# Windowed attention and feed-forward on one core: chunks of 384 tokens, split zero fill and a new order of work

## The chip, the core and the metric

One core of a Trainium2 chip runs the whole computation. Its engines are TensorE (PE in the profile; its weight loads are PEld), VectorE (DVE), ScalarE (ACT) and GpSimd (POOL); DMA queues are started by SyncE (SP) and ACT. The metric is device time in microseconds. Before the change it is 338.51 us, the median of three runs (337.94 to 339.54). Runs are compared in the fast state only, unless a slow one is named as such. "Granted clock" is the share of TensorE's full clock that the trace records.

## The reference

```python
# q, k, v: 8 batches x 8 heads x 576 tokens x 64, fp32; w_in 512 x 2048, w_out 2048 x 512
scores = scale * q @ k.T
rel    = pos[:, None] - pos[None, :]
plain  = (rel >= 0) & (rel < 32)                        # heads 0 to 3
dil    = (rel >= 0) & (rel < 128) & (rel % 4 == 0)      # heads 4 to 7
attn   = softmax(where(mask, scores, -1e9))
x      = (attn @ v).transpose(0, 2, 1, 3).reshape(4608, 512)
h      = x @ w_in
out    = maximum(0.01 * h, h) @ w_out                   # 4608 x 512, fp32
```

## The kernel before

The kernel is a list of steps, `PROGRAM`, and a loop that emits the instructions of each step. No scheduler reorders them: every engine gets its own share of the list in that order, with waits for data and buffers. In the trace ACT's 276 exponentials, logarithms and evictions start in just that order. The steps that matter here:

- `lq`, `lv`, `lw` load q and k, v, and a quarter of a weight matrix; `cq`, `cv`, `cw` cast them to fp16 on DVE (`V`), ACT (`A`) or GpSimd (`P`).
- `B` transposes q and k on PE; `T` does it by DMA (from group 5 on).
- `S:u` computes the scores of attention unit `u` and their exponential; `M:u` multiplies by the mask (a step `S:u:b` adds a bias on PE instead); `D:u` computes values and denominators and writes the normalised result to xT.
- `I:c:j` is one tile of the first feed-forward layer of token chunk `c`; `O:t:g` is a quarter of the second layer of 128-token tile `t`.
- `Z:n` multiplies a zero tile n times: fillers where the author expected PE to wait.

There are 16 groups of three units: half a batch (four heads) in two units of two heads x 384 tokens, and one unit of four heads x the last 192 tokens.

```python
psa = ...tile_pool(name="psa", bufs=1, space=PSUM)    # sps (2 banks), o, den
psm = ...tile_pool(name="psm", bufs=4, space=PSUM)    # tag pm: hp, op, tp
CHUNKS = [(0, 384), (384, 192), (576, 448)] + [(1024 + 512 * i, 512) for i in range(7)]
RING = 2048       # tokens that xT holds
GRING = 1024      # tokens that gt holds
...
def values(u, log_recip=False, pool=None):
    if pool is None:
        o   = psa.tile([128, 512], FP32, tag="o")
        den = psa.tile([128, 512], FP32, tag="den")
    else:                                  # "p": borrow two of the four pm banks
        den = pool.tile([128, 512], FP32, tag="pm")
        o   = pool.tile([128, 512], FP32, tag="pm")
    ...                                    # den matmuls, o matmuls
    if log_recip:                          # "l": logarithm, then exponential, on ACT
        nc.scalar.activation(out=ln, in_=den, func=AF.Ln)
        nc.scalar.activation(out=rec, in_=ln, func=AF.Exp, scale=-1.0)
    else:                                  # "r"
        nc.vector.reciprocal(out=rec, in_=den)
    ...                                    # xT = o * rec on DVE, cut in two where the ring wraps

def ff_in(c, j):
    hp = psm.tile([128, 512], FP32, tag="pm")
    for i in range(4):
        nc.tensor.matmul(hp[:, 0:w], w1[j // 4][:, i, j % 4::4], xT[:, i, x0:x0 + w], ...)
    nc.scalar.activation(out=gt[:, j, g0:g0 + w], in_=hp[:, 0:w], func=AF.Prelu, alpha=0.01)

def ff_out(t, g):                          # the tile stays open from g == 0 to g == 3
    if g == 0:
        ops[t] = psm.tile([128, 512], FP32, tag="pm")
    for j in range(4 * g, 4 * g + 4):
        nc.tensor.matmul(ops[t], gt[:, j, g0:g0 + 128], w2[g][:, j % 4, :], ...)
    if g == 3:
        nc.scalar.copy(out=ob, in_=ops[t])
        nc.scalar.dma_start(out[128 * t:128 * t + 128, :], ob)
```

The softmax here doesn't subtract the row's maximum and nothing guards it: scores larger than these inputs give would overflow.

## Time and profile before

| | before |
|---|---|
| time | 338.51 us |
| span of the profiled run (whose time is 339.5 us) | 337.6 us |
| PE, ACT, DVE, POOL busy | 97%, 51%, 51%, 28% |
| filler matmuls | 59, 21.8 us busy |
| first feed-forward matmul at | 27.4 us |
| first second-layer matmul at | 76.4 us |
| DMA busy in the first 28 us, and from 28 to 64 us | 93%, 96% |

PE is nearly always busy, so its stream decides the time. The question to put to such a profile isn't whether PE is busy but with what. Fillers count as busy, and the prediction takes them apart. One view more belongs here: the timeline of PE just before the first group of chunk 2 (start, length, engine, line, operation, tiles, count, and in brackets the wait).

```profile
57.07 0.35 PE L281 MATMUL den<-em,ones 80*64 80x384 f16 x2 [0.62 <-DVE em L265]
...
58.59 0.82 PE L396 MATMUL wp<-xT 128*128 128x512 f16 x2
59.47 0.35 PE L281 MATMUL den<-em,ones 128*64 128x384 f16 x2
...
61.26 0.35 PE L281 MATMUL den<-em,ones 128*64 128x384 f16 x2
61.80 0.36 PE L289 MATMUL o<-em,vh 128*64 128x96 f16 x8 [0.18 <-DVE xT L313]
...
62.37 1.47 PE L396 MATMUL wp<-xT 128*128 128x512 f16 x4
63.68 1.11 PE L343 MATMUL hp<-xT,w 128*128 128x448 f16 x5
```

Between 56.5 and 63.7 us PE has little real work. The last three attention units of chunk 2 (11, 9 and 8) stand there one behind the other in the single pair of banks `o` and `den`, some 2 us apart, and the product of the last one ends at 63.4 us. It isn't their values that are late: those had landed by 38.6 us and were cast by 44.2. At that moment not one second-layer matmul has been issued, although chunks 0 and 1 have gone through the first layer; the quarter of w_out that the program uses first lands last, at 62.6 us.

### The profile page before, as it was taken

Reading aid. Unit: us, or ns where it says so; the run is one execution under the profiler, and the core shown is the slowest. Engines: PE = TensorE matmul, PEld = TensorE weight load, DVE = VectorE, ACT = ScalarE, POOL = GpSimd, SP = SyncE. Lnnn points to the kernel's source line nnn. Section 1 sums busy time; section 2 is a strip of 40 time slices with the busy share of each in tenths; the row PEclk is TensorE's granted clock in tenths of the full one; section 3 lists DMA queues with packets and bytes.
Section 4 is the critical chain, followed back from the end, with each engine's and each line's share of the span. In section 5 each row is a group of like instructions: output and inputs, shape, how many; then the busy total and the mean of one; then the engine's idle time right before and its main releaser. Section 6 shows DMA issues by size and latency. Waiting matters only on the chain.

```text
span 337.6 us, 6297 instructions
## 1 busy us (share of the span) xinstructions
PE 326.7 (97%) x2639; PEld 168.6 (50%) x2639; DVE 173.0 (51%) x190; ACT 171.3 (51%) x293; POOL 95.0 (28%) x93
## 2 busy tenths in 40 slices
PE   7999898999999899999999999999999999999995
...
DMA  6999899790499399999669945700110020011011
GB/s 208 287 392 376 285 292 337 177 193 31 135 261 283 86 234 242 227 288 222 155 166 242 212 107 162 174 3 0 64 62 2 8 85 33 0 62 64 0 57 67
DMA packets 111243, 53.02 MB, mean 157 GB/s; under 512 B 96880, under 2 KB 101488, under 8 KB 110704
## 3 DMA queue, kind: packets, MB, share of 16 engines
...
## 4 chain that ended last, share of the span: by engine, by line
PE 90%; DVE 5%; issue 1%; DMA 1%; ACT 1%; DVEq 0%
PE op L353 36%; PE hp L343 34%; PE wp L396 6%; PE sps L255 6%; PE den L281 4%; PE o L289 2%; PE tp L206 2%; DVE rec L297 2%; DVE em L265 2%; DMA out_dram<-ob 1%; DVE xT L313 1%; PE sps L243 1%; ACT ln L294 0%; ACT ob L357 0%; DVE vh L189 0%
## 5 line engine op out<-in xcount | busy, mean ns | idle before, releaser
L343 PE MATMUL hp<-xT,w 128*128 128x512 f16 (+3 forms) x640 | 130.9, 359 | 0.0
L353 PE MATMUL op<-w,gt 128*128 128x512 f16 x576 | 128.8, 379 | 0.0
L345 ACT ACTIVATE gt<-hp 128x512 f16<-128x512 f32 (+3 forms) x160 | 88.0, 554 | 43.0 <-PE hp L343 42.3
L297 DVE RECIPROCAL rec<-den 128x384 f32<-128x384 f32 x32 | 81.8, 2557 | 42.5 <-PE den L281 42.5
L343 PEld LDWEIGHTS <-w 128*128 128x128 f16 x640 | 68.9, 114 | 52.8 <-issue 1.2
L353 PEld LDWEIGHTS <-gt 128*128 128x128 f16 x576 | 54.9, 98 | 64.6
L357 ACT COPY ob<-op 128x512 f32<-128x512 f32 x36 | 21.1, 587 | 82.3 <-PE op L353 82.3
L313 DVE TENSOR_TENSOR xT<-o,rec 128x192 f16<-128x192 f32 (+3 forms) x72 | 34.6, 508 | 34.1 <-ACT rec L295 30.8
L258 ACT ACTIVATE er<-sps 128x768 f16<-128x768 f32 (+1 forms) x48 | 38.8, 808 | 24.0 <-PE sps L255 21.9
L265 DVE TENSOR_TENSOR em<-er,mask 128x768 f16<-128x768 f16 (+1 forms) x42 | 30.8, 736 | 2.2 <-ACT er L258 2.2
L396 PE MATMUL wp<-xT 128*128 128x512 f16 x59 | 21.8, 420 | 3.2 <-DVE xT L112 1.3
L189 POOL CAST vh<-vf 128x2048 f16<-128x2048 f32 (+1 forms) x8 | 13.5, 1682 | 39.5 <-PE o L289 21.6
L176 POOL CAST qh<-qf 96x768 f16<-96x768 f32 x16 | 14.3, 921 | 36.2 <-DMA qf<-in_q_dram 35.9
L255 PEld LDWEIGHTS <-kT 64*128 64x128 f16 (+1 forms) x448 | 14.8, 121 | 17.0 <-issue 16.1
L255 PE MATMUL sps<-qT,kT 64*128 64x96 f16 (+1 forms) x448 | 22.9, 229 | 0.0
L176 POOL CAST kh<-kf 96x768 f16<-96x768 f32 x20 | 17.6, 904 | 5.0 <-DMA kf<-in_k_dram 4.3
L289 PEld LDWEIGHTS <-vh 128*64 128x64 f16 (+1 forms) x448 | 15.8, 110 | 3.4 <-DVE xT L313 0.7
L281 PE MATMUL den<-em,ones 128*64 128x384 f16 (+1 forms) x84 | 14.8, 349 | 2.4 <-DVE em L265 2.2
L185 POOL CAST vh<-vf 128x1536 f16<-128x1536 f32 x6 | 9.0, 1503 | 28.1 <-PE o L289 22.8
L330 POOL CAST w<-wf 128x2048 f16<-128x2048 f32 x7 | 13.9, 1983 | 7.4 <-DMA wf<-in_moe_w_out_dram 4.3
L289 PE MATMUL o<-em,vh 128*64 128x96 f16 (+1 forms) x392 | 14.8, 201 | 0.6 <-DVE xT L313 0.6
L281 PEld LDWEIGHTS <-ones 128*64 128x64 f16 (+1 forms) x96 | 5.7, 106 | 11.0 <-issue 6.7
...
## 6 DMA issues: line engine op xcount, KB each, us to landing
...
```

Of the source, the lines that this page charges most:

```text
L176: eng(out=t[0:96, 12 * D * p:12 * D * p + 12 * D].rearrange("p (t h d) -> p h t d", t=6, h=2), in_=f[0:96, 12 * p:12 * p + 12, :].rearrang ...
L255: nc.tensor.matmul(sps[0:kp, hh, w * x:w * x + w], ka, qa, start=not pe_mask, stop=not pe_mask or x == len(tiles) - 1)
L258: nc.scalar.activation(out=er[0:kp], in_=sps[0:kp, :, 0:384], func=AF.Exp, scale=SCALE)
L265: nc.vector.tensor_tensor(out=em[0:kp].rearrange("p h (t c) -> p h t c", c=w), in0=er[0:kp].rearrange("p h (t c) -> p h t c", c=w), in1=ba ...
L281: nc.tensor.matmul(den[64 * hh:64 * hh + 64, 0:384], ones[0:kp], em[0:kp, hh, :], start=True, stop=True)
L289: nc.tensor.matmul(o[64 * hh:64 * hh + 64, w * x:w * x + w], vt[0:kp, sl, :], em[0:kp, hh, w * x:w * x + w], start=True, stop=True)
L297: nc.vector.reciprocal(out=rec, in_=den[:, 0:384])
L313: nc.vector.tensor_tensor(out=out_x, in0=ins[0], in1=ins[1], op=ALU.mult)
L343: nc.tensor.matmul(hp[:, 0:w], w1[j // 4][:, i, j % 4::4], xT[:, i, x0:x0 + w], start=(i == 0), stop=(i == 3))
L345: nc.scalar.activation(out=gt[:, j, g0:g0 + w], in_=hp[:, 0:w], func=AF.Prelu, alpha=0.01)
L353: nc.tensor.matmul(op, gt[:, j, g0:g0 + 128], w2[g][:, j % 4, :], start=(j == 0), stop=(j == 15))
L396: nc.tensor.matmul(wp, warm[:, 0:128], warm, start=True, stop=True)
```

## The change

Its intent: chunks of 384 tokens instead of 512, with xT as a ring of exactly four batches so that no product is cut at the wrap; the zero fill of buffers split over engines; and the whole list of steps laid out again, by an author who wanted it to hold up under several assumptions about durations.

```diff
-CHUNKS = [(0, 384), (384, 192), (576, 448)] + [(1024 + 512 * i, 512) for i in range(7)]
-RING = 2048
-GRING = 1024
+CHUNKS = [(0, 384), (384, 192), (576, 384), (960, 192)] + [(1152 + 384 * i, 384) for i in range(9)]
+RING = 2304
+GRING = 1152
 PROGRAM (cut to the part between chunk 1 and chunk 2):
-I:1:15 D:11:l Z:1 S:14:m Z:1 Z:1 D:9:l S:13:m Z:1 Z:1 cv:4:P:b cq:5:k:P:b D:8:l S:12:m
-Z:2 cw:1:0:P Z:1 Z:1 I:2:0
+D:6:lp M:11 D:8:lp D:7:r S:10:m O:0:0 I:1:7 ... I:1:12 M:10 I:1:13 lv:3:b lw:1:3 O:1:0 O:0:1
+O:1:1 cv:3:V:b I:1:14 lq:4:b O:2:0 O:2:1 ... I:1:15 cq:4:k:P:b O:0:2 D:11:l O:1:2 ... O:0:3
+D:10:l O:1:3 O:2:2 B:4:0:AV D:9:l B:4:1:VV S:12:m ... T:5 O:2:3 O:3:0 I:2:0
 ... (the rest of PROGRAM is all new)
-    qT = [cst.tile([128, PAD + 2 * S], FP16) ...]
+    qT = [cst.tile([128, 2 * S], FP16) ...]
-    nc.vector.memset(vf[0][0:32], 0.0)
-    for h in range(4):
-        nc.vector.memset(vf[1][64:128, 8 * h + 4:8 * h + 8, :], 0.0)
+    nc.vector.memset(vf[1].rearrange(...)[64:128, :, 1, :], 0.0)
+    nc.scalar.copy(out=vf[0][0:32]..., in_=warm[0:32]...)            # zeros, on ACT
+        nc.vector.memset(t[:, S:PAD + S], 0.0)                      # for each kT
     values(): the loop over the two pieces of a wrapped product is gone
```

Counted over the list: fillers 59 to 35; first-layer groups 160 to 208, second-layer groups 144 in both; units with a DVE reciprocal 32 to 9; units that borrow `pm` banks for values 4 to 21; value casts on GpSimd 14 of 18 to 7 of 16; weight casts on GpSimd 7 of 8 to 3 of 8.

More of the change, by code (lines that the diff above doesn't have):

```diff
@@ L19 @@
 NTOK = B * S
-CHUNKS = [(0, 384), (384, 192), (576, 448)] + [(1024 + 512 * i, 512) for i in range(7)]
-RING = 2048
-GRING = 1024
+CHUNKS = [(0, 384), (384, 192), (576, 384), (960, 192)] + [(1152 + 384 * i, 384) for i in range(9)]
+RING = 2304
+GRING = 1152
 NEG = -30000.0
 PROGRAM = """
-Z:2 Z:2 mask Z:1 lq:1:0 Z:2 Z:1 Z:1 lq:0:0 cq:0:q:V:0 Z:2 lv:1:0 Z:1 lq:1:1 Z:1 lq:0:1 cq:0:k:A:0
-cq:1:k:P:0 Z:4 lv:0:0 cv:1:P:0 Z:2 B:0:0:VA Z:1 cq:1:k:P:1 lv:0:1 Z:1 cq:1:q:V:0 lw:0:0 cq:1:q:V:1
-Z:1 cq:0:k:P:1 cq:0:q:P:1 lv:1:1 lq:2:b Z:1 S:0:b cv:1:P:1 lq:3:b Z:2 cw:0:0:P B:1:0:AA Z:3 Z:1
@@ L30 @@
-cv:0:V:0 Z:1 lw:0:1 S:3:b B:0:1:VA cq:3:k:P:b cw:0:1:P B:1:1:AV cv:0:V:1 Z:1 Z:2 lw:0:2 S:1:b Z:2
-Z:1 D:3:lp S:4:b Z:1 D:0:lp cw:0:2:P D:1:lp Z:3 lw:0:3 S:2:b D:4:lp cq:2:q:A:b Z:2 S:5:b Z:1 Z:1
-cq:2:k:V:b Z:1 lv:2:b I:0:0 lv:3:b lq:4:b I:0:1 I:0:2 B:2:0:AA cq:3:q:V:b B:2:1:AV cw:0:3:P Z:1 Z:1
-D:5:l B:3:0:VA S:6:m lw:1:1 Z:1 Z:1 I:0:3 Z:1 B:3:1:VA lw:1:2 S:9:m D:2:l cv:3:P:b I:0:4 M:6
-cv:2:V:b I:0:5 I:0:6 S:10:m I:0:7 M:9 I:0:8 I:0:9 lq:5:b I:0:10 lv:4:b M:10 I:0:11 I:0:12 I:0:13
-I:0:14 S:7:m D:6:r I:0:15 M:7 I:1:0 I:1:1 cq:4:q:P:b I:1:2 I:1:3 I:1:4 cq:4:k:V:b I:1:5 cw:1:1:P
@@ L36 @@
-S:8:m I:1:6 cw:1:2:P I:1:7 I:1:8 lw:1:3 I:1:9 D:7:l lw:1:0 I:1:10 S:11:m lq:6:b B:4:0:VV D:10:l M:11
-I:1:11 B:4:1:AV I:1:12 I:1:13 M:8 I:1:14 I:1:15 D:11:l Z:1 S:14:m Z:1 Z:1 D:9:l S:13:m Z:1 Z:1
-cv:4:P:b cq:5:k:P:b D:8:l S:12:m Z:2 cw:1:0:P Z:1 Z:1 I:2:0 I:2:1 cq:5:q:V:b T:5 lv:5:b cq:6:k:P:b
-I:2:2 I:2:3 I:2:4 I:2:5 I:2:6 I:2:7 I:2:8 I:2:9 lv:6:b M:12 I:2:10 I:2:11 cw:1:3:V D:12:r cv:5:P:b
-I:2:12 I:2:13 I:2:14 I:2:15 O:0:0 O:0:1 O:0:2 O:0:3 O:1:0 O:1:1 M:14 O:1:2 O:1:3 O:2:0 S:16:m D:14:l
@@ L41 @@
-O:2:1 M:13 O:2:2 cq:6:q:V:b T:6 lq:7:b O:2:3 O:3:0 O:3:1 S:17:m M:16 M:17 D:16:l lq:8:b O:3:2 O:3:3
-S:15:m D:13:l O:4:0 O:4:1 M:15 O:4:2 O:4:3 O:5:0 cv:6:P:b O:5:1 O:5:2 O:5:3 O:6:0 D:15:l S:18:m
-O:6:1 lv:7:b O:6:2 lv:8:b O:6:3 O:7:0 M:18 O:7:1 cq:7:k:V:b S:19:m D:18:r cv:7:V:b O:7:2 O:7:3 I:3:0
-M:19 I:3:1 D:17:l I:3:2 cq:7:q:A:b T:7 lq:9:b lv:9:b I:3:3 I:3:4 S:20:m D:19:r M:20 cq:8:q:P:b
-cq:8:k:P:b cv:8:P:b I:3:5 I:3:6 I:3:7 I:3:8 I:3:9 S:21:m D:20:r M:21 T:8 I:3:10 I:3:11 I:3:12 I:3:13
-I:3:14 S:22:m D:21:r M:22 lq:10:b lv:10:b I:3:15 O:8:0 O:8:1 O:8:2 O:8:3 S:23:m D:22:r M:23
@@ L47 @@
-cq:9:q:P:b cq:9:k:P:b cv:9:P:b O:9:0 O:9:1 O:9:2 O:9:3 O:10:0 S:24:m D:23:r M:24 T:9 O:10:1 O:10:2
-O:10:3 O:11:0 S:25:m D:24:r M:25 lq:11:b lv:11:b O:11:1 O:11:2 O:11:3 I:4:0 I:4:1 S:26:m D:25:r M:26
-cq:10:q:P:b cq:10:k:P:b cv:10:P:b I:4:2 I:4:3 I:4:4 I:4:5 I:4:6 S:27:m D:26:r M:27 T:10 I:4:7 I:4:8
-I:4:9 I:4:10 I:4:11 S:28:m D:27:r M:28 lq:12:b lv:12:b I:4:12 I:4:13 I:4:14 I:4:15 O:12:0 S:29:m
-D:28:r M:29 cq:11:q:P:b cq:11:k:P:b cv:11:P:b O:12:1 O:12:2 O:12:3 O:13:0 S:30:m D:29:r M:30 T:11
@@ L52 @@
-O:13:1 O:13:2 O:13:3 O:14:0 O:14:1 S:31:m D:30:r M:31 lq:13:b lv:13:b O:14:2 O:14:3 O:15:0 O:15:1
-O:15:2 S:32:m D:31:r M:32 cq:12:q:P:b cq:12:k:P:b cv:12:P:b O:15:3 I:5:0 I:5:1 I:5:2 I:5:3 S:33:m
-D:32:r M:33 T:12 I:5:4 I:5:5 I:5:6 I:5:7 I:5:8 S:34:m D:33:r M:34 lq:14:b lv:14:b I:5:9 I:5:10
-I:5:11 I:5:12 S:35:m D:34:r M:35 cq:13:q:P:b cq:13:k:P:b cv:13:P:b I:5:13 I:5:14 I:5:15 O:16:0
-O:16:1 S:36:m D:35:r M:36 T:13 O:16:2 O:16:3 O:17:0 O:17:1 O:17:2 S:37:m D:36:r M:37 lq:15:b lv:15:b
-O:17:3 O:18:0 O:18:1 O:18:2 O:18:3 S:38:m D:37:r M:38 cq:14:q:P:b cq:14:k:P:b cv:14:P:b O:19:0
@@ L58 @@
-O:19:1 O:19:2 O:19:3 I:6:0 S:39:m D:38:r M:39 T:14 I:6:1 I:6:2 I:6:3 I:6:4 S:40:m D:39:r M:40 I:6:5
-I:6:6 I:6:7 I:6:8 I:6:9 S:41:m D:40:r M:41 cq:15:q:P:b cq:15:k:P:b cv:15:P:b I:6:10 I:6:11 I:6:12
-I:6:13 I:6:14 S:42:m D:41:r M:42 T:15 I:6:15 O:20:0 O:20:1 O:20:2 S:43:m D:42:r M:43 O:20:3 O:21:0
-O:21:1 O:21:2 O:21:3 O:22:0 S:44:m D:43:r M:44 O:22:1 O:22:2 O:22:3 O:23:0 S:45:m D:44:r M:45 O:23:1
-O:23:2 O:23:3 I:7:0 I:7:1 S:46:m D:45:r M:46 I:7:2 I:7:3 I:7:4 I:7:5 I:7:6 S:47:m D:46:r M:47 I:7:7
@@ L63 @@
-I:7:8 I:7:9 I:7:10 D:47:r I:7:11 I:7:12 I:7:13 I:7:14 I:7:15 O:24:0 O:24:1 O:24:2 O:24:3 O:25:0
-O:25:1 O:25:2 O:25:3 O:26:0 O:26:1 O:26:2 O:26:3 O:27:0 O:27:1 O:27:2 O:27:3 I:8:0 I:8:1 I:8:2 I:8:3
-I:8:4 I:8:5 I:8:6 I:8:7 I:8:8 I:8:9 I:8:10 I:8:11 I:8:12 I:8:13 I:8:14 I:8:15 O:28:0 O:28:1 O:28:2
-O:28:3 O:29:0 O:29:1 O:29:2 O:29:3 O:30:0 O:30:1 O:30:2 O:30:3 O:31:0 O:31:1 O:31:2 O:31:3 I:9:0
-I:9:1 I:9:2 I:9:3 I:9:4 I:9:5 I:9:6 I:9:7 I:9:8 I:9:9 I:9:10 I:9:11 I:9:12 I:9:13 I:9:14 I:9:15
-O:32:0 O:32:1 O:32:2 O:32:3 O:33:0 O:33:1 O:33:2 O:33:3 O:34:0 O:34:1 O:34:2 O:34:3 O:35:0 O:35:1
@@ L69 @@
-O:35:2 O:35:3
+Z:3 lq:1:1 Z:8 lq:0:1 Z:2 cq:0:q:V:1 cq:1:k:A:1 Z:1 lq:0:0 lq:1:0 cq:1:q:P:1 lv:1:b Z:3 cq:0:k:A:1
+B:1:1:VV Z:5 cq:0:q:V:0 Z:1 B:0:1:AA cq:1:k:P:0 Z:2 cq:1:q:V:0 Z:2 S:4:b B:1:0:VA lv:0:b lq:2:b
+S:1:b lw:0:0 Z:1 cv:1:V:b cq:0:k:P:0 lq:3:b B:0:0:AA lw:0:1 S:3:b D:4:rp S:0:b D:3:lp cq:2:q:V:b Z:3
+S:2:b Z:1 cv:0:P:b lw:0:2 D:0:lp cq:2:k:P:b D:1:l S:5:b B:2:1:AV B:2:0:VA cq:3:k:V:b Z:2 D:2:lp
+cw:0:0:P lw:0:3 lv:2:b Z:1 cq:3:q:P:b S:7:m D:5:l mask S:6:m cw:0:1:V lw:1:0 I:0:0 I:0:1 M:7
@@ new lines @@
+B:3:0:AA S:8:m B:3:1:AV I:0:2 I:0:3 S:9:b I:0:4 cw:0:2:V I:0:5 I:0:6 M:6 I:0:7 S:11:m M:8 I:0:8
+I:0:9 I:0:10 cw:0:3:V lw:1:1 I:0:11 I:0:12 I:0:13 cv:2:P:b cw:1:0:V I:0:14 I:0:15 cw:1:1:P lw:1:2
+I:1:0 I:1:1 I:1:2 I:1:3 I:1:4 cw:1:2:P I:1:5 I:1:6 D:6:lp M:11 D:8:lp D:7:r S:10:m O:0:0 I:1:7 I:1:8
+I:1:9 I:1:10 I:1:11 I:1:12 M:10 I:1:13 lv:3:b lw:1:3 O:1:0 O:0:1 O:1:1 cv:3:V:b I:1:14 lq:4:b O:2:0
+O:2:1 cq:4:q:P:b cw:1:3:V lv:4:b lq:5:b I:1:15 cq:4:k:P:b O:0:2 D:11:l O:1:2 lq:6:b O:0:3 cq:6:q:P:b
@@ new lines @@
+D:10:l O:1:3 O:2:2 B:4:0:AV D:9:l B:4:1:VV S:12:m cq:5:q:V:b cq:5:k:V:b T:5 O:2:3 O:3:0 I:2:0 I:2:1
+I:2:2 I:2:3 I:2:4 I:2:5 I:2:6 I:2:7 S:14:m I:2:8 I:2:9 I:2:10 I:2:11 cv:4:A:b cq:6:k:V:b O:3:1
+I:2:12 lv:5:b T:6 M:14 O:3:2 I:2:13 M:12 lq:7:b O:3:3 I:2:14 lv:6:b cv:5:P:b I:2:15 I:3:0 I:3:1
+I:3:2 O:4:0 I:3:3 I:3:4 S:13:m I:3:5 I:3:6 O:4:1 I:3:7 I:3:8 I:3:9 M:13 I:3:10 I:3:11 I:3:12 I:3:13
+S:15:m D:12:r D:13:lp O:5:0 cq:7:q:P:b M:15 O:4:2 I:3:14 S:16:m M:16 cq:7:k:P:b T:7 lv:7:b lq:8:b
+lq:9:b D:14:l O:5:1 O:4:3 S:17:m D:16:lp D:15:l I:3:15 cv:7:P:b M:17 O:5:2 O:6:0 O:6:1 I:4:0 O:5:3
@@ new lines @@
+I:4:1 S:19:m O:6:2 O:7:0 O:7:1 O:6:3 O:7:2 I:4:2 I:4:3 D:17:l S:20:m cq:9:k:P:b O:8:0 I:4:4 S:18:m
+I:4:5 M:20 O:8:1 I:4:6 O:7:3 O:8:2 S:21:m I:4:7 cv:6:V:b I:4:8 M:18 M:19 D:20:lp S:22:m M:21 D:18:r
+I:4:9 I:4:10 O:8:3 I:4:11 I:4:12 I:4:13 M:22 cq:8:k:V:b D:19:lp S:23:m D:22:lp D:21:l I:4:14 I:4:15
+O:9:0 O:10:0 I:5:0 O:9:1 O:9:2 cq:8:q:V:b T:8 lv:8:b O:9:3 I:5:1 I:5:2 O:11:0 O:10:1 I:5:3 O:11:1
+I:5:4 O:10:2 I:5:5 I:5:6 M:23 O:10:3 cq:9:q:P:b T:9 lq:10:b lq:11:b lv:9:b I:5:7 I:5:8 S:25:m D:23:l
@@ new lines @@
+I:5:9 O:11:2 I:5:10 I:5:11 I:5:12 I:5:13 I:5:14 M:25 I:5:15 I:6:0 I:6:1 O:12:0 I:6:2 O:12:1 S:26:m
+O:11:3 I:6:3 I:6:4 I:6:5 cv:8:V:b I:6:6 S:28:m O:12:2 O:12:3 S:24:m cq:10:q:P:b I:6:7 I:6:8 I:6:9
+O:13:0 cq:11:q:A:b I:6:10 I:6:11 O:13:1 M:28 S:27:m cq:11:k:P:b D:25:r I:6:12 I:6:13 cq:10:k:A:b
+T:10 lv:10:b I:6:14 O:13:2 cv:9:P:b lv:11:b T:11 lq:12:b lq:13:b I:6:15 O:14:0 O:13:3 O:14:1 M:24
+O:15:0 D:28:l S:29:m M:27 O:14:2 O:14:3 O:16:0 cq:12:k:P:b O:15:1 D:27:l D:24:lp S:30:m O:16:1
+O:15:2 O:15:3 I:7:0 I:7:1 I:7:2 I:7:3 I:7:4 M:29 I:7:5 I:7:6 cv:10:P:b O:16:2 cq:12:q:P:b T:12
@@ new lines @@
+lv:12:b lq:15:b M:26 O:16:3 O:17:0 M:30 S:33:m D:29:lp D:26:l cv:11:V:b lv:13:b S:34:m M:33 I:7:7
+O:17:1 I:7:8 I:7:9 I:7:10 I:7:11 M:34 I:7:12 I:7:13 I:7:14 D:33:r S:32:m cq:13:q:A:b O:17:2 D:34:lp
+S:31:m O:17:3 M:31 I:7:15 O:18:0 O:18:1 D:30:lp D:31:l S:35:m M:35 O:18:2 O:19:0 O:18:3 I:8:0 I:8:1
+I:8:2 I:8:3 I:8:4 cq:13:k:P:b T:13 lq:14:b S:38:m I:8:5 I:8:6 I:8:7 I:8:8 I:8:9 O:19:1 I:8:10 I:8:11
+I:8:12 O:19:2 I:8:13 I:8:14 I:8:15 M:32 O:20:0 S:36:m M:38 D:35:rp D:32:l S:37:m O:19:3 O:20:1
+O:20:2 cv:12:V:b cv:13:P:b M:37 O:21:0 O:20:3 O:22:0 cq:14:q:V:b cq:15:k:A:b M:36 O:21:1 O:22:1
@@ new lines @@
+I:9:0 I:9:1 D:38:l S:40:m O:21:2 I:9:2 M:40 O:21:3 I:9:3 cq:15:q:P:b T:15 lv:14:b I:9:4 I:9:5 I:9:6
+D:37:l D:40:rp S:39:m O:22:2 I:9:7 S:41:m D:36:l I:9:8 O:22:3 O:23:0 I:9:9 O:23:1 cq:14:k:P:b T:14
+lv:15:b I:9:10 O:23:2 M:39 I:9:11 O:23:3 D:39:l S:47:m I:9:12 I:9:13 I:9:14 I:9:15 M:41 I:10:0
+I:10:1 O:24:0 O:24:1 M:47 I:10:2 S:46:m I:10:3 O:24:2 I:10:4 O:25:0 S:45:m cv:15:V:b D:41:l D:47:lp
+S:42:m O:25:1 I:10:5 cv:14:V:b O:25:2 I:10:6 M:42 M:46 O:24:3 I:10:7 I:10:8 M:45 I:10:9 S:43:m
+D:45:lp D:46:l O:26:0 M:43 I:10:10 O:25:3 I:10:11 I:10:12 S:44:m D:43:r D:42:lp I:10:13 O:26:1
@@ new lines @@
+I:10:14 I:10:15 O:26:2 O:26:3 I:11:0 I:11:1 I:11:2 O:27:0 I:11:3 I:11:4 I:11:5 I:11:6 M:44 O:27:1
+O:27:2 O:27:3 D:44:lp I:11:7 I:11:8 O:28:0 I:11:9 I:11:10 I:11:11 O:29:0 I:11:12 O:28:1 I:11:13
+O:29:1 O:28:2 I:11:14 I:11:15 O:29:2 O:28:3 I:12:0 I:12:1 I:12:2 I:12:3 O:30:0 O:30:1 O:29:3 I:12:4
+O:30:2 O:31:0 O:30:3 I:12:5 I:12:6 I:12:7 I:12:8 I:12:9 I:12:10 O:32:0 O:31:1 I:12:11 I:12:12 O:31:2
+I:12:13 O:31:3 O:32:1 I:12:14 I:12:15 O:33:0 O:32:2 O:34:0 O:32:3 O:33:1 O:34:1 O:35:0 O:33:2 O:34:2
@@ L70 @@
+O:33:3 O:35:1 O:34:3 O:35:2 O:35:3
 """
@@ L115 @@
     NPE = 5
-    qT = [cst.tile([128, PAD + 2 * S], FP16, name=f"qT{i}") for i in range(NB)]
+    qT = [cst.tile([128, 2 * S], FP16, name=f"qT{i}") for i in range(NB)]
     kT = [cst.tile([128, PAD + 2 * S], FP16, name=f"kT{i}") for i in range(NB)]
@@ L121 @@
     vf = [cst.tile([128, 24, D], FP32, name="vf0"), cst.tile([128, 32, D], FP32, name="vf1")]
+    nc.vector.memset(vf[1].rearrange("p (h a r) d -> p h a (r d)", a=2, r=4)[64:128, :, 1, :], 0.0)
+    nc.scalar.copy(out=vf[0][0:32].rearrange("p (a t) d -> p a (t d)", a=3),
+                   in_=warm[0:32].unsqueeze(1).to_broadcast([32, 3, 512]))
     for t in kT:
         nc.vector.memset(t[:, 0:PAD], 0.0)
-    nc.vector.memset(vf[0][0:32], 0.0)
+        nc.vector.memset(t[:, S:PAD + S], 0.0)
     nc.vector.memset(vf[1][0:32], 0.0)
-    for h in range(4):
-        nc.vector.memset(vf[1][64:128, 8 * h + 4:8 * h + 8, :], 0.0)
     def rows_ap(x, off, ap):
@@ L195, in transpose @@
         for nm, dst in (("q", qT), ("k", kT)):
-            o = dst[n % NB][:, PAD:PAD + 2 * S].rearrange("p (c r) -> p c r", r=96)
+            o = dst[n % NB][:, -2 * S:].rearrange("p (c r) -> p c r", r=96)
             nc.sync.dma_start_transpose(o, qkh[n, nm][0:96, :])
@@ L206, in pe_transpose @@
                 nc.tensor.transpose(tp[r, 64 * t:64 * t + 64], h[r, t, :], ident[r, r])
-        o = (qT if nm == "q" else kT)[n % NB][:, PAD + S * p:PAD + S * p + S]
+        o = (qT if nm == "q" else kT)[n % NB][:, -2 * S:][:, S * p:S * p + S]
         eng(out=o.rearrange("p (r t) -> p r t", t=9),
@@ L250, in scores @@
                     ka = kT[n % NB][r, tok - 128 + j: tok - 128 + j + 4 * kp - 3: 4]
-                    qa = qT[n % NB][r, tok + j: tok + j + 4 * w - 3: 4]
+                    qa = qT[n % NB][r, tok - PAD + j: tok - PAD + j + 4 * w - 3: 4]
                 else:
                     ka = kT[n % NB][r, tok + 96 * j - 32: tok + 96 * j + 96]
-                    qa = qT[n % NB][r, tok + 96 * j: tok + 96 * j + 96]
+                    qa = qT[n % NB][r, tok - PAD + 96 * j: tok - PAD + 96 * j + 96]
                 nc.tensor.matmul(sps[0:kp, hh, w * x:w * x + w], ka, qa, start=not pe_mask,
```

19 lines of the change are left out of this document (6 added, 13 removed).

## The prediction

> **What bounds the kernel now.** I read the engine totals first, then the slices of the span, then the chain that ended last in order of time, then groups by form, and last the timeline of PE. Engine totals and two rows of the slices:
>
> ```profile
> PE 326.7 (97%) x2639; PEld 168.6 (50%) x2639; DVE 173.0 (51%) x190; ACT 171.3 (51%) x293; POOL 95.0 (28%) x93
> ...
> PE   7999898999999899999999999999999999999995
> ...
> DMA  6999899790499399999669945700110020011011
> ```
>
> PE has work almost everywhere, and the other engines are half idle, so PE's stream sets the end. The holes in PE's row lie in the first fifth, where DMA is full. But 97% busy isn't 97% useful. The groups by form (busy, mean of one, idle before):
>
> ```profile
> L353 PE MATMUL op<-w,gt 128*128 128x512 f16 x576 | 128.8, 379 | 0.0
> L343 PE MATMUL hp<-xT,w 128*128 128x512 f16 x448 | 101.1, 380 | 0.0
> L297 DVE RECIPROCAL rec<-den 128x384 f32<-128x384 f32 x32 | 81.8, 2557 | 42.5 <-PE den L281 42.5
> L345 ACT ACTIVATE gt<-hp 128x512 f16<-128x512 f32 x112 | 66.8, 597 | 35.6 <-PE hp L343 34.9
> L396 PE MATMUL wp<-xT 128*128 128x512 f16 x59 | 21.8, 420 | 3.2 <-DVE xT L112 1.3 <-ACT ln L294 0.3
> L345 ACT ACTIVATE gt<-hp 128x384 f16<-128x384 f32 x16 | 7.7, 490 | 2.4 <-PE hp L343 2.4
> ```
>
> The 59 `wp` matmuls are fillers: they multiply a zero tile where the author expected PE to wait. 21.8 us of the busy time is therefore idleness in disguise. The means of 380 ns are latencies of overlapping matmuls; the pace is read from the chain (start, length, what), where 64 matmuls without interruption take 13.81 us, 215.8 ns each:
>
> ```profile
> 264.96 13.81 PE op L353 x64
> 278.77 13.81 PE hp L343 x64
> ...
> 334.06 0.59 ACT ob L357
> ```
>
> The last line also gives the tail: the span is 337.6 us, so eviction and store after PE's last group cost 3.5 us. The timeline around 121 us shows what an attention unit costs PE between feed-forward matmuls:
>
> ```profile
> 120.76 0.52 PE L255 MATMUL sps<-qT,kT 64*128 64x96 f16 x8
> ...
> 121.22 0.35 PE L281 MATMUL den<-em,ones 128*64 128x384 f16 x2
> ...
> 121.40 0.34 PE L289 MATMUL o<-em,vh 128*64 128x96 f16 x8
> ...
> 121.67 2.56 PE L343 MATMUL hp<-xT,w 128*128 128x512 f16 x11
> ```
>
> From start to start, the undisturbed cases of scores plus values lengthen the feed-forward stream by 0.82 us (1.26 with the 16 score matmuls of an odd third unit). Scores alone cost 0.37 and values alone 0.55 at their cheapest, so a split pair costs 0.1 more.
>
> Adding the start-to-start times of all matmuls: useful feed-forward 249 us; fillers 21.8; some 7 us of real waits, nearly all before 117 us. The longest late one is here, where values wait for the mask product, which ran beside GpSimd casts (1.66 us, against 0.55 where GpSimd rests):
>
> ```profile
> 113.55 1.66 DVE L265 TENSOR_TENSOR em<-er,mask 128x768 f16<-128x768 f16 x1
> ...
> 115.26 0.35 PE L281 MATMUL den<-em,ones 128*64 128x384 f16 x2 [0.88 <-DVE em L265]
> ```
>
> So at most about 29 us of the span is reclaimable without removing arithmetic. The rest is matmuls.
>
> [...]215.8 ns at 512, 162 to 163 at 384, 83 at 192 (medians, start to start). [...]here four `pm` banks serve projections, outputs and transposes, and no feed-forward group in the trace waits over 31 ns for one. [...]
>
> **The change, part by part.**
>
> *Chunks.* Before, 64 times (7 x 215.8 + 162.5 + 189 + 83) = 124.5 us of first-layer matmuls. After, 64 times (11 x 162.5 + 2 x 83) = 125.0 us: +0.5. Second layer unchanged, 576 x 215.8 = 124.3. ACT evicts 176 tiles at 490 and 32 at 329 ns = 96.8 us instead of 88.0. The gain meant is earlier starts: a chunk no longer waits for as many tokens, and the ring of 2304 holds whole batches, so the products that wrapped are not cut (72 become 64; DVE work off the path).
>
> *Reciprocals.* 32 on DVE become 9; logarithm with exponential on ACT goes from 16 to 39 units. DVE loses 23 x 2.56 = 59 us, ACT gains 23 x 1.01 = 23 us. The path from `den` to xT shortens by 1.5 us, and 21 of 48 units take two of the four `pm` banks for it (before, 4).
>
> *Casts.* GpSimd: 14 value casts become 7, seven weight casts 3; DVE and ACT take the rest. A DVE weight cast is 1.2 us against 2.0. ACT's sum rises to about 215 us (66%), DVE's falls to about 145, GpSimd's to about 60.
>
> *Fillers.* 59 become 35, all ahead of the first feed-forward group. The new program has no filler afterwards, whereas the old one has 14 there (5.2 us).
>
> *Order.* Before, second-layer groups begin at 76.5 us, after the third chunk. After, they begin during the second chunk, near 45 us, and fill the time in which weights and values arrive. Summing DMA bytes in the new queue order at the 270 GB/s that q, k, v got and the 400 that weights got: first w_in quarter lands at 21.5 us, last at 34, first w_out quarter at 38, third value block at 45. Each cast then finishes before the program asks for it. Transposes by DMA stand 10 us or more ahead of their scores.
>
> *Zero fill.* One 32-partition fill of 1.34 us moves from DVE to ACT, idle then; three small key fills are added. The first real PE work stays bound by loads (9.9 us before, my estimate 9 after).
>
> *Head.* Before, the first feed-forward matmul starts at 27.4 us, with 6 scores, 4 values and 4 transpose pairs done. After, the program does 8, 6 and 6 first. Following its longest dependence: values 1 land near 13, their DVE casts end near 19, then D of unit 4 with a 2.56 us reciprocal; its banks come free near 23 for unit 0; two more ln/exp pairs and products, then the DVE evictions of two transposes, near 28. Estimate 29 us for the first feed-forward matmul.
>
> *Body.* From there: 125.0 + 124.3 + 0.9 of small excess. Attention left: 40 scores, 42 values, 4 transpose pairs in 40 interruptions instead of 45. Twelve scores alone x 0.37, ten pairs x 0.82, seven threes x 1.28, and the mixed ones come to 37.3; odd third units add 3.5 and one bias mask 0.4: 41.3 us. Sum 291.5; tail 3.9 with the last matmul. Span without waits: 29 + 291.5 + 3.9 = 324.4. The time exceeds the span by 0.9 (338.5 against 337.6): 325.3. The same sum for the old body is 45 us of attention, and its 56.8 measured are that plus 5.2 of fillers plus 6.5 of waits.
>
> *New waits.* Walking the program with four banks: before, a second-layer tile was filled in one go. Now 160 of 208 first-layer groups run with one or more output tiles open, so three banks or fewer rotate. With three of 384 columns there is 1.30 us between the end of a bank's fill and its reuse; eviction needs about 0.25 + 0.49 + release, some 0.85, and an Exp of 0.81 in front of it makes 1.65. About twenty places have under 1.0 us. ACT's sum over ten microseconds of PE work reaches ten in three places (near 25, 65 and 185). I allow 3 us in all, with a range of 1 to 9. That gives 328.5.
>
> **Rivals.** (1) The fillers only marked real waiting for loads, and removing them leaves bare gaps: then the head moves later by some 5 us and the time is 333 to 337. For it: DMA is at 93% in the first 27 us. Against: second-layer work now fills in. (2) ACT becomes the local bound through open tiles and ln/exp: 40 interruptions each losing 0.3 us make 12 us, 337, same. For it: strict order and 66%. Against: ACT has eviction slack in every second-layer stretch (2.87 us idle between its copies). (3) The order works as its author planned, with a head near 25 and almost no waits: 320 to 322.
>
> **Range and chances.** Floor 325.3 with my head, 321 with the best head; 335 with rivals 1 and 2 in part. 2% faster is 331.7, which leaves 3.2 us above my estimate, about the size of my error in the head plus waits. Faster 0.72, same 0.27, slower 0.01.
>
> **What would show it.** Right: `wp` x35; `hp` x832 at 162 ns pace; first `hp` near 29 us, first `op` near 45; PE waits on ACT evictions (a line absent before) totalling 1 to 9 us; reciprocals x9, DVE near 145 us; last `op` near 324. Wrong: a first `hp` after 33 (rival 1); `hp` or `op` waits on ACT above 9 us, or ACT full in slices past 60 us (rival 2); waits for `em` or casts growing because DVE and GpSimd collide; attention costing over 45 us in the body.

## The result and the profile after

The changed kernel takes 326.5 us (median of four runs, 325.37 to 328.24) beside 338.88 us for the kernel before (median of four). The ratio is 0.9641, with a 95% interval of 0.9584 to 0.9698. Ratios here are the mean time of one kernel's fast runs over that of the other's of the same rounds, so not quite the ratio of the medians quoted. Two of the four runs have a granted clock of 0.998 to 0.999 and take 325.4 and 325.6; the other two have 0.992 and 0.993 and take 328.2 and 327.4. The profiled run is of the first kind; its span is 323.7 us against 337.6.

Engine totals and three rows of the slices (tenths busy, 40 slices of 8.1 us):

```profile
PE 316.3 (98%) x2809; PEld 186.4 (58%) x2809; DVE 121.7 (38%) x173; ACT 203.0 (63%) x395; POOL 61.6 (19%) x66
...
PE   8989999999999999999999999999999999999995
...
ACT  4589792688765783667747787557765774544412
...
DMA  7999898998979107992099669909610000001012
```

The holes of PE's row that lay in the first fifth are gone after the third slice. ACT has taken over work from DVE, but of its slices only the fourth and the sixth are full. DMA is as full at the start as before.

The groups by form that answer to those of before:

```profile
L349 PE MATMUL op<-w,gt 128*128 128x512 f16 x576 | 137.3, 379 | 0.0
L339 PE MATMUL hp<-xT,w 128*128 128x384 f16 x704 | 126.9, 327 | 0.0
L341 ACT ACTIVATE gt<-hp 128x384 f16<-128x384 f32 x176 | 83.5, 490 | 50.4 <-PE hp L339 48.1 <-ACT ob L353 0.9 <-PE sps L258 0.4
L300 DVE RECIPROCAL rec<-den 128x384 f32<-128x384 f32 x9 | 23.0, 2554 | 19.7 <-PE den L284 19.7
L392 PE MATMUL wp<-xT 128*128 128x512 f16 x35 | 11.9, 448 | 1.7 <-DVE xT L114 1.3
```

The 576 second-layer matmuls have risen from 128.8 to 137.3 us of busy time although nothing about them changed. That is an artefact of how overlapping matmuls are added: now that groups alternate between layers, more of each group's start and end is counted. Start to start, the same 576 take 126.0 us before and 126.1 after. This is why the accounts below use starts and not busy times.

Adding start-to-start times of all matmuls in both traces, in us:

| | before | after | difference |
|---|---|---|---|
| fillers | 21.8 | 11.5 | -10.3 |
| first layer, its waits included | 129.1 | 127.7 | -1.5 |
| second layer, its waits included | 126.0 | 126.1 | +0.1 |
| attention, transposes, bias, their waits included | 55.4 | 53.1 | -2.3 |
| first to last matmul | 332.3 | 318.3 | -14.0 |

What takes the fillers' place shows in a view of the busy time between 28 and 64 us, cut to the second layer's tiles (stretch, its length, busy time with count of PE and ACT, clock, DMA share, GB/s). Before:

```profile
28.00:64.00 36.00, 0.00 (x0) 0.00 (x0) 1.00 0.96 298
```

After:

```profile
28.00:64.00 36.00, 12.41 (x52) 1.74 (x3) 1.00 0.96 303
```

In the same 36 us, with the same clock, DMA share and rate, the old kernel issues no second-layer matmul and the new one issues 52, or 13 groups: 11.2 us at 215.8 ns each. The first group of chunk 2 starts at 63.7 us before and 63.3 us after. So both kernels get there at the same moment, and the new one has 11.2 us of the rest behind it. They get there for different reasons: in the new order of loads three quarters of w_out land before the values of group 3 (41.1, 43.6 and 46.3 us), and those values land at 48.3 us instead of 38.6 and are cast by 52.4.

Its waits on PE, all of them (who waited for whom, us in total, times, longest):

```profile
PE wp L392 <- DVE xT L114: 1.3, 1, 1.3
PE tp L209 <- issue: 0.8, 1, 0.8
PE sps L246 <- ACT er L261: 0.7, 2, 0.5
PE sps L258 <- ACT er L261: 0.5, 1, 0.5
```

All four lie before the first feed-forward group or at it (27.5 us). After it the profile lists no wait of PE at all.

### The profile page after: what moved, and what is told of

It reads as the page before. It is cut to its first block, busy times and chain, and to the rows that moved or that the text cites. A ratio compares the mean times of both kernels' runs of the same rounds, so it can differ in the third digit from the quotient of the medians.

```text
span 323.7 us, 6683 instructions
## 1 busy us (share of the span) xinstructions
PE 316.3 (98%) x2809; PEld 186.4 (58%) x2809; DVE 121.7 (38%) x173; ACT 203.0 (63%) x395; POOL 61.6 (19%) x66
## 4 chain that ended last, share of the span: by engine, by line
PE 96%; ACT 2%; issue 0%; DVE 0%
PE hp L339 39%; PE op L349 39%; PE sps L258 6%; PE den L284 4%; PE wp L392 3%; PE o L292 3%; PE tp L209 2%; ACT er L261 1%; PE sps L246 1%; ACT ob L353 0%; ACT qT L211 0%; ACT kT L211 0%; ACT rec L298 0%; ACT ln L297 0%; DVE xT L114 0%
## 5 line engine op out<-in xcount | busy, mean ns | idle before, releaser
L339 PE MATMUL hp<-xT,w 128*128 128x384 f16 (+1 forms) x832 | 138.8, 314 | 0.0
L349 PE MATMUL op<-w,gt 128*128 128x512 f16 x576 | 137.3, 379 | 0.0
L341 ACT ACTIVATE gt<-hp 128x384 f16<-128x384 f32 (+1 forms) x208 | 93.5, 465 | 57.5 <-PE hp L339 55.2
L339 PEld LDWEIGHTS <-w 128*128 128x128 f16 x832 | 89.2, 114 | 42.8 <-issue 0.9
L309 DVE TENSOR_TENSOR xT<-o,rec 128x384 f16<-128x384 f32 (+1 forms) x64 | 33.6, 553 | 93.3 <-ACT rec L298 91.9
L261 ACT ACTIVATE er<-sps 128x768 f16<-128x768 f32 (+1 forms) x48 | 38.6, 804 | 8.7 <-PE sps L258 7.5
L268 DVE TENSOR_TENSOR em<-er,mask 128x768 f16<-128x768 f16 (+1 forms) x41 | 25.6, 646 | 23.7 <-ACT er L261 23.4
L300 DVE RECIPROCAL rec<-den 128x384 f32<-128x384 f32 x9 | 23.0, 2554 | 19.7 <-PE den L284 19.7
L297 ACT ACTIVATE ln<-den 128x384 f32<-128x384 f32 x39 | 18.9, 485 | 5.2 <-PE den L284 3.9
L298 ACT ACTIVATE rec<-ln 128x384 f32<-128x384 f32 x39 | 20.4, 524 | 1.2
L179 POOL CAST qh<-qf 96x768 f16<-96x768 f32 x12 | 12.1, 1032 | 35.8 <-DMA qf<-in_q_dram 35.7
L192 POOL CAST vh<-vf 128x2048 f16<-128x2048 f32 x4 | 7.6, 1892 | 38.8 <-PE o L292 23.6
L392 PE MATMUL wp<-xT 128*128 128x512 f16 x35 | 11.9, 448 | 1.7 <-DVE xT L114 1.3
```

The costliest lines, as they stand in the source:

```text
L179: eng(out=t[0:96, 12 * D * p:12 * D * p + 12 * D].rearrange("p (t h d) -> p h t d", t=6, h=2), in_=f[0:96, 12 * p:12 * p + 12, :].rearrang ...
L261: nc.scalar.activation(out=er[0:kp], in_=sps[0:kp, :, 0:384], func=AF.Exp, scale=SCALE)
L268: nc.vector.tensor_tensor(out=em[0:kp].rearrange("p h (t c) -> p h t c", c=w), in0=er[0:kp].rearrange("p h (t c) -> p h t c", c=w), in1=ba ...
L300: nc.vector.reciprocal(out=rec, in_=den[:, 0:384])
L309: nc.vector.tensor_tensor(out=out_x, in0=ins[0], in1=ins[1], op=ALU.mult)
L349: nc.tensor.matmul(op, gt[:, j, g0:g0 + 128], w2[g][:, j % 4, :], start=(j == 0), stop=(j == 15))
```

## The experiments

My theory after the result: in the changed kernel the pace is set by the arrivals while q, k, v and weights arrive (to about 63 us). The new order puts second-layer work there that the old one had left for later; that is most of the gain. The rivals are that the gain comes from the shorter chain of the reciprocal and the lighter DVE (rival A), from dropping fillers that held the stream up (rival B), from the casts' move off GpSimd, or from the zero fill.

Each experiment also had runs of the kernel before beside it (337.2 to 341.5 us).

### Second-layer work taken out of the time of loading

```diff
 after, PROGRAM: the 16 O steps before I:2:15 (13 of them before I:2:0)
-... O:0:0 ... O:1:0 O:0:1 ... O:3:0 I:2:0 ... I:2:15
+... I:2:0 ... I:2:15 O:0:0 O:1:0 O:0:1 ... O:3:3
```

> The changed kernel with its first 16 second-layer groups (13 of them stood before the first group of chunk 2) moved behind the last first-layer group of chunk 2; all else as it is. Theory (the gain is second-layer work put into the time in which values and weights arrive): in the changed kernel the first chunk-2 group starts at 63.3 us with 11.2 us of second-layer work already done; without that work PE would be there at 52 us, but the value cast ends at 52.4 and the key transposes of unit 12 at about 59, so PE waits until some 60 us. Loss 7 to 9 us, time near 334, with the waits of PE on DVE and casts between 48 and 60 us in the trace. Rival A (the gain is the shorter reciprocal and mask chains, order matters little): loss under 2 us.

It took 334.78 us (four runs, 334.05 to 336.54; ratio to before 0.9905, interval 0.9861 to 0.9949). That is 8.3 us more than the changed kernel, two thirds of the whole gain, undone by starting the second layer at 74.0 us instead of 45.5. The longest waits of PE:

```profile
PE o L290 <- DVE vh L193: 3.4, 1, 3.4
PE o L290 <- DVE xT L307: 1.5, 1, 1.5
...
PE op L347 <- ACT gt L339: 1.2, 1, 1.2
```

The first of them is the one expected: values wait for the value cast, at 52 us. The waits aren't all. The clock falls too, as the busy time of two stretches shows (length; PE, PEld, DVE, ACT, POOL; then the clock):

```profile
51.90:54.80 2.90, 0.31 (x2) 0.06 (x1) 2.86 (x4) 1.04 (x3) 2.06 (x2) 1.00 0.78 166
54.80:61.70 6.90, 4.55 (x114) 3.65 (x116) 5.18 (x7) 2.66 (x5) 2.52 (x3) 0.51 0.93 211
```

From 54.8 us on, still in the hole of 3.8 us (51.9 to 55.7), the granted clock is 0.5 for nearly 6.9 us. So this wait cost more than its length. All four runs of this kernel show a mean clock of 0.985 to 0.990. The first group of chunk 2 starts at 61.9 us instead of 63.3, but the two traces can't be compared by these times: this run, the slowest of the four, is already 2.4 us late at its first feed-forward matmul (30.0 against 27.5 us), after a half-clock stretch from 24.1 to 27.5 us, where both programs are still the same. Counted from the first feed-forward matmul, chunk 2 comes after 31.9 us instead of 35.8. So with 11.2 us of work taken out PE gets there 3.9 us sooner, and the other 7.3 us are lost when the work is done later: most of the 8.3.

### Second-layer work put into the kernel before

```diff
 before, PROGRAM (w_out quarters renumbered so that the first one loaded is quarter 0):
-D:11:l Z:1 S:14:m Z:1 Z:1 D:9:l S:13:m Z:1 Z:1 ... D:8:l S:12:m Z:2 cw:1:0:P Z:1 Z:1 I:2:0
+D:11:l O:0:0 S:14:m O:0:1 D:9:l S:13:m O:1:0 ... D:8:l S:12:m O:1:1 cw:1:3:P I:2:0
 (O:0:2 O:0:3 O:1:2 O:1:3 follow after I:2:11; nothing else moves)
```

> The kernel before with four second-layer groups (3.45 us) in place of the nine fillers between chunk 1 and chunk 2; the w_out quarters are renumbered so that the quarter loaded first is the one used first. Theory: those fillers stood on real waits, so the work is free there: 2.5 to 3.5 us faster than before, near 335.5. Rival A: no gain, since the chains of chunk 2 set the start of its first group and PE only idles elsewhere; or the two open tiles leave two banks for 512 columns and cost what was won: within 1 us of before.

333.48 us (332.56 to 335.80; ratio 0.9868, interval 0.9808 to 0.9927): 4.7 us faster than the before of the same rounds (338.17). The interval is about 2.5 to 6.5 us, so the 3.45 us of work that was moved lie within it. The timeline of PE:

```profile
55.05 0.35 PE L279 MATMUL den<-em,ones 80*64 80x384 f16 x2
...
58.53 1.04 PE L351 MATMUL op<-w,gt 128*128 128x512 f16 x4
...
60.72 1.04 PE L351 MATMUL op<-w,gt 128*128 128x512 f16 x4
61.59 4.59 PE L341 MATMUL hp<-xT,w 128*128 128x448 f16 x23
```

Chunk 2 starts at 61.6 us instead of 63.7 although real work stands where fillers stood. But this lead of 2.1 us isn't the edit's. It is there before the first replaced filler: 0.6 us at the first feed-forward matmul (26.8 against 27.4), 2.0 at unit 11's `den` (55.05 here, 57.07 in the view of the kernel before). Over the stretch where work replaces fillers it doesn't grow. So in these two traces the work that was moved is free, as expected, and the rest is the difference between two executions.

### All reciprocals back on DVE, and its two halves

```diff
 after, PROGRAM, all 39 units with "l" (21 in their own banks, 18 in borrowed ones):
-D:4:rp ... D:3:lp ... D:1:l
+D:4:rp ... D:3:rp ... D:1:r
```

> The changed kernel with all 39 logarithm-exponential reciprocals made DVE reciprocals (2.56 us each) again; order unchanged. Theory: DVE rises from 122 to some 221 us busy of 290, still below PE, but a value's banks are held 1.5 us longer and products come later: 2 to 5 us slower, near 330. Rival A: the shortened chain is most of the gain, then 8 to 12 us slower, near 337.

383.64 us (382.55 to 385.17): 57 us slower than the changed kernel, far outside what either theory gave. DVE is only 56% busy, so its average says nothing. The two halves were sent later to find out why. The first:

```diff
 after, PROGRAM, the 21 units in their own banks:
-D:1:l
+D:1:r
```

> Splits the 57 us that all 39 reciprocals on DVE cost. Here only the 21 units that use their own two banks take the DVE reciprocal; the 18 that borrow feed-forward banks keep logarithm and exponential. Theory (a borrowed bank held 1.5 to 4 us longer is what starves the first layer): 3 to 12 us slower than the changed kernel, 330 to 338. Rival (DVE is overloaded in bursts, wherever the banks lie): about 21 of 39 parts of the loss, 31 us, near 357.

338.35 us (337.44 to 341.71), 12 us slower than the changed kernel: just above the upper end of what I had said (338).

The second:

```diff
 after, PROGRAM, the 18 units in borrowed banks:
-D:3:lp
+D:3:rp
```

> The other half: only the 18 units that borrow feed-forward banks take the DVE reciprocal. Theory (held banks): most of the 57 us, 30 to 45 us slower, 357 to 371, with waits of first-layer groups on the reciprocal and half-clock stretches after them. Rival (DVE bursts): about 18 of 39 parts, 26 us, near 352; both halves then add up to the whole.

358.35 us (357.78 to 359.91), 32 us slower, with fewer units changed: 1.8 us per unit against 0.6. The longest waits on PE of the second half:

```profile
PE hp L337 <- DVE rec L298: 10.2, 4, 3.4
```

and of the first half:

```profile
PE hp L337 <- DVE xT L307: 4.7, 6, 1.6
```

In the borrowed half first-layer groups wait for the reciprocal itself: they need nothing from it but the bank in which `den` stands. Where two values follow each other, the second bank is held for both reciprocals, 2.56 us each, with a product between. In the other half the waits are for xT, mostly data. Half-clock stretches follow in the borrowed half (mean clock 0.966 to 0.969, against 0.99 and above in the other): 23.9 us of them in its trace, which make up to 12 of its 32 us. Some of its waits are for DVE and not for a bank, the longest a transpose that waits 2.9 us for a cast. And the two sets of units stand at different places of the list. So held banks look like the larger part of the loss, but the division isn't clean. The halves add up to 44 us, not 57; the remaining 13 appear only when both are slow, and I did not take them apart.

### Reciprocals moved to ACT in the kernel before

```diff
 before, PROGRAM: all 32 units
-D:6:r
+D:6:l
```

> The kernel before with its 32 DVE reciprocals made logarithm and exponential on ACT. Theory: PE hardly waits for them there (one wait of 0.4 us behind a reciprocal near 259 us, some in 45 to 62 us): 0 to 1.5 us faster, near 338. Rival A: 5 us or more faster.

336.31 us (335.74 to 338.91; ratio 0.9957, interval 0.9907 to 1.0008). Some 1.9 us by the medians, a verdict of same, with an interval that touches 1. The move whose undoing costs 57 us in the new order is worth little in the old one. As the cause of most of the gain, rival A falls.

### No borrowed banks

```diff
 after, PROGRAM: the 21 units with "p"
-D:3:lp
+D:3:l
```

> The changed kernel with all values in their own two banks instead of 21 units borrowing two of the four pm banks. Thirteen places have two values next to each other; the second then waits for the logarithm (1 us after den) and for the product (2 us). Theory: the borrowing is a condition of the new order, so 8 to 20 us slower, with PE waits on ACT and DVE at den and o. Rival (the banks were never tight): within 2 us.

371.56 us as a median of four, one of them slow; the three fast ones take 369.93 to 372.97. That is over 43 us slower, more than twice the upper end of what I expected. The waits on PE:

```profile
PE o L290 <- DVE xT L307: 14.6, 19, 1.3
PE den L282 <- DVE rec L298: 10.1, 5, 2.5
PE den L282 <- ACT ln L295: 5.0, 9, 0.9
```

Thirty-three waits of about 0.9 us on average, 29.7 us in all: values that follow another closely find the one pair of banks taken. And again the mean clock falls, to 0.958 to 0.965 in the fast runs.

### No fillers after the head, in the kernel before

```diff
 before, PROGRAM: the 14 fillers after I:0:0
-Z:1
```

> The kernel before without the 14 filler matmuls (5.2 us) that come after its first feed-forward group. Theory: they cover real waits, so taking them out leaves bare gaps: same time within 1 us. Rival B (the fillers themselves held the stream up): up to 5 us faster, near 334.

341.73 us (341.58 to 342.08; ratio 1.0084, interval 1.0037 to 1.0130). Neither theory said this: taking useless matmuls out makes the kernel 3 us slower. The clock shows how:

```profile
36.40:39.80 3.40, 3.40 (x24) 1.73 (x21) 1.23 (x4) 2.59 (x5) 1.63 (x1) 0.50 0.91 253
...
63.70:67.10 3.40, 3.08 (x9) 1.32 (x9) 3.06 (x6) 1.11 (x2) 2.93 (x1) 0.50 0.93 209
```

Two stretches of 3.4 us run at half clock. The first follows a stop of PE at 33 us (2.8 us, where the old kernel has one of 1.1), the second the bare gaps between 57 and 64 us. From start to start the first layer's matmuls take 132.6 us instead of 129.1, and attention with fillers takes 0.8 us less: the two stretches, up to 1.7 us each, are the loss. The fillers didn't hold up the stream; without them it lost clock. Which of the 14 matter isn't shown. Rival B falls, and so does my reading of them as free.

### No fillers at all, in the changed kernel

```diff
 after, PROGRAM: all 35 fillers
-Z:3 lq:1:1 Z:8 lq:0:1 Z:2 cq:0:q:V:1 ...
+lq:1:1 lq:0:1 cq:0:q:V:1 ...
```

> The changed kernel without its 35 fillers, all of which stand before its first feed-forward group. Theory: loads set the pace of the head, so the fillers cost nothing, and the clock is the question: [...]the work of the head is slower and the first feed-forward group comes 0 to 2 us later: 326 to 329. Rival B: 1 to 3 us faster.

The three fast runs take 324.24, 324.50 and 326.72; one slow run took 329.98 with a clock of 0.984. The ratio to before, 0.9607 (0.9529 to 0.9685), doesn't differ from the changed kernel's. That the work of the head would be slower had not been tested before this run. In the profiled run it is: PE is slow until 18.0 us (18 transposes take 0.69 us before, 0.45 to 0.47 after; the run's mean granted clock of 0.999 shows nothing of it), and the first feed-forward group still starts sooner than with fillers (26.1 against 27.5 us). In the first 12 us the transposes wait 7.1 us for casts, and no cost of the slow array shows.

### Casts back on GpSimd

```diff
 after, PROGRAM: nine value casts, five weight casts
-cv:1:V:b  cv:4:A:b  cw:0:1:V
+cv:1:P:b  cv:4:P:b  cw:0:1:P
```

> The changed kernel with all value and w casts on GpSimd (nine value casts and five weight casts move back). Theory: the casts are on the path while data arrive (27 to 62 us): a weight cast takes 0.7 us longer, and queued casts come later still; slack there is 1 to 4 us, so 2 to 6 us slower. Rival (casts are hidden): within 1 us.

328.03 us (327.39 to 331.43; ratio 0.9698, interval 0.9632 to 0.9765): 1.5 us by the medians, with an interval that overlaps that of the changed kernel. The first feed-forward matmul of the profiled run comes at 30.7 us instead of 27.5, but that run is the slowest of the four (331.43) and has a half-clock stretch at 18.5 us. The effect is small and not clear of the spread.

### The old zero fill

```diff
 after:
-    nc.scalar.copy(out=vf[0][0:32]..., in_=warm[0:32]...)
+    nc.vector.memset(vf[0][0:32], 0.0)
     (and the strided fill of vf[1] in four parts again)
```

> The changed kernel with the zero fill of the value buffers as it was before, all on DVE (the ACT copy gone, one fill of 1.34 us back on DVE, the strided fill in four parts again). Theory: the head waits for loads, and DVE's first cast waits until its data at about 6.9 us anyway: within 1 us of the changed kernel, 325 to 328. Rival (DVE's fills delay the first cast and thereby everything): 1 to 2 us slower.

325.98 us (six runs, 324.65 to 326.29; ratio 0.9599, interval 0.9566 to 0.9633): no difference from the changed kernel. The split zero fill, one of the named parts of the change, is worth nothing measurable.

### An attempt at a better version

```diff
 after, PROGRAM:
-lq:2:b ... lw:0:0 ...              cq:2:k:P:b D:1:l S:5:b B:2:1 B:2:0 ... I:0:0 I:0:1 ... I:0:2 I:0:3
+lw:0:0 lq:2:b ... cw:0:0:P ...     cq:2:k:P:b D:1:l S:5:b I:0:0 I:0:1 I:0:2 I:0:3 B:2:1 B:2:0 ...
```

> An attempt at a better version: in the changed kernel the first w_in quarter is loaded and cast before unit 2's q and k, the first four first-layer groups stand before the transposes of unit 2, and the three fillers after them are gone. Theory: everything after is 0.9 us sooner, until weights and values arrive just in time, and the 1.0 us hole at 23 us between two transposes, [...]is covered by long matmuls: 1 to 2 us faster than the changed kernel, 324 to 325.5. Rival (the head is bound by bytes loaded): same, or a later q and k push the transposes out: 0 to 3 us slower.

A miss. The first feed-forward matmul does come at 23.9 us instead of 27.5, but the two fast runs take 326.18 and 326.97, and four of six runs are slow, 331.8 to 332.3 at a clock of 0.984 to 0.985. In the profiled one, which is slow, the stretches from 23.7 to 27.1 and from 34.0 to 40.8 us run at half clock. The fast runs gain nothing either. My reading is that starting sooner only means meeting the next arrivals sooner; no fast run was traced to show it. The changed kernel stays the best of those that I have tried beside the one without fillers, from which it doesn't differ.

## Why the prediction was right

The measured 326.5 us lies in the range of 321 to 335, 2.0 us below the point of 328.5. Step by step:

**The bound and the reclaimable part.** It put the reclaimable part of the span at about 29 us, fillers and waits together. Of it 14.0 us were reclaimed, 10.3 of them as fillers that are no longer there.

**Chunks.** It had +0.5 us of first-layer matmuls. The pace came out as computed (medians start to start: 163 ns at 384, 83 at 192), and the sum with waits fell by 1.5 us. The chunk size was never isolated, since the ring, the chunks and the order only work together; that it helps by itself is open.

**Order.** It said that second-layer work would begin near 45 us, in the time of arrivals. It began at 45.45. This step carries the result: undoing it costs 8.3 of 12.4 us, and adding a piece of it to the old kernel gives 4.7. What the other 4 us come from was not taken apart.

**Reciprocals.** "The path from `den` to xT shortens by 1.5 us" was listed as if it were a gain of its own. It isn't (1.9 us in the old kernel, unclear). In the new order it is a condition: undoing it costs 57 us, and undoing the borrowing of banks 43. The prediction counted how many units borrow but asked only whether first-layer groups would starve with the chain as short as it is.

**Head.** Estimated 29 us, measured 27.5. The value casts of unit group 1 ended at 16.5 us, not 19: the second of the pair took 0.69 us, where I had taken the figure of one that ran beside GpSimd.

**Body.** Attention after the first feed-forward group: estimated 41.3 us, measured 42.1, with all waits in it. The 0.82 us of a pair was the cheapest case of the old trace: the median of its 23 is 1.00, and so is the pair that the prediction shows. In the new trace the interruptions fell near the cheap values, which was luck in part.

**New waits.** Estimated 3 us; hardly 1 appears (the 42.1 just named hold them). ACT's three crowded places were survived. The 0.25 us between a bank's fill and its eviction was an estimate: in the trace before, with ACT idle, an eviction starts 0.20 us after the last matmul's 215.8 ns (median of 103 of 512 columns), and the 0.49 of 384 columns came out as taken. That a whole Exp stands in an eviction's way was an estimate too: of the 15 first-layer evictions of the new trace that follow an Exp at once, the latest starts 0.29 us after the end of its last matmul, against a median of 0.04 with ACT idle. The sum of head, body, tail and waits was 327.4 for the span; the trace has 323.7, of which the head and the waits explain 3.5.

**Time over span.** Taken as 0.9 us, in the profiled run 1.7. The 0.9 was a misreading: it set the median time beside the span of a run that took 339.5 us, and that run's difference is 1.9. There is a slip of 0.2 as well, since 325.3 and 3 make 328.3 and not 328.5. Two of the four timed runs take 2 to 3 us longer at a lower clock, a term that the prediction does not have at all. That these errors partly offset a head and waits put too high is luck.

**Other sums.** ACT estimated 215 us, measured 203; GpSimd 60 against 61.6; DVE 145 against 121.7. Value casts on DVE took 2.0 to 2.1 us a pair, where the old trace has 3.1, and the mask products of 128x768 took 0.65 us instead of 0.75. A quieter GpSimd fits: in the old trace these products take 0.54 to 0.57 us where GpSimd rests and up to 1.72 beside its casts, and with the casts back on it (95.0 us busy instead of 61.6) the same 34 products take 0.92.

**The rivals.** Rival 1 (bare gaps in the head) and rival 2 (ACT as local bound) did not come about. What neither foresaw is what a gap does to the clock. The prediction called fillers "idleness in disguise". In the old kernel's later part the 14 of them earn 3 us.

## What to carry to other kernels

While transfers set the pace, look for work of a later stage whose inputs are already there, and put it into the gaps; the start of the next stage then moves little, but more is done by then. Before shortening such a gap in another way, test whether it is one: take the later work out and see if the stage that follows starts sooner (here by 3.9 us for 11.2 us of work removed, half clock included). Check where a difference between two traces begins: two executions were over 2 us apart before the first edited step. And judge a buffer by how long it is held, not by how many use it: two of four banks borrowed for a chain of 1 us left no wait of PE after the head, and in 18 units the same two held for 2.6 us cost 32 us, lost clock included.

## What the traces leave open

- What brings the clock down. A stretch in which no two matmuls start more than 1.53 us apart (the kernel before without late fillers; PE idle for 3.0 of the 7.3 us from 56.4 to 63.7 us) was followed by half clock, while a single pause of 1.76 us (the changed kernel with the old zero fill, mean clock 0.998) was not, and a half-clock stretch began inside one of 1.43 us (second layer late, 24.1 us). What decides between them isn't shown. Stretches at a granted clock of 0.50 and 0.51 lasted 3.4 us in the first of these runs (36.4 to 39.8 and 63.7 to 67.1 us) and up to 6.9 us in the last (54.8 to 61.7 us).
- What fillers are worth. In the changed kernel without fillers PE was slow until 18.0 us (0.69 us for 18 transposes), although it was busy for 10.8 of these 18 us, mostly with small matmuls. It cost nothing that the runs show (the first feed-forward matmul came 1.4 us sooner). So fillers earned nothing in the new kernel's head, and 14 of them earned 3 us in the old kernel's later part.
- Why PE stops between transposes. In the traces of four kernels PE stops for 1.0 to 3.0 us between two small transposes, with nothing in the profile that it waits for, at 23 us (changed kernel), 35 us (before), 33 us (before without late fillers) and 34 us (the attempt at a better version). Each time an instruction transfer of 16,384 bytes started between 1.5 us before and 0.3 us after the stop began (22.0, 33.8, 33.3 and 33.3 us). The changed kernel's trace has 22 such transfers and one such stop. That the transfer is the cause is a reading of the coincidence, not a test.
